# Attention numerators with the query features as stationary operand, tails and query projections in strips

## The chip, the cores and the metric

The kernel runs on one core of one Trainium2 chip. The metric is the device time of one execution in microseconds (us); the kernel before has a median of 1146.33 us over three runs.

## What is computed

Linear attention with positive random features for 8 batches of 8 heads (576 tokens, head size 64, 128 projected features), then a gated feed-forward network (FFN) over the 4608 tokens that come out:

```python
def phi(x):                                   # 64 -> 128 -> 256 features
    proj = einsum('bhsd,df->bhsf', x, w_phi)
    proj = proj - max(abs(proj), axis=-1, keepdims=True)
    return concatenate([exp(proj), exp(-proj)], axis=-1)
q_p, k_p = phi(q), phi(k)
kv  = einsum('bhsf,bhsd->bhfd', k_p, v)       # the sums
z   = sum(k_p, axis=2)
num = einsum('bhsf,bhfd->bhsd', q_p, kv)      # the numerators
den = einsum('bhsf,bhf->bhs', q_p, z)[..., None] + 1e-06
x   = (num / den) laid out as 4608 tokens x 512
out = (silu(x @ w_gate) * (x @ w_val)) @ w_out     # 512 -> 1536 -> 512
```

## The kernel before

**Order of work.** Every piece of work is a `Step` with an engine, an estimated cost, a rank and the PSUM banks that it takes and gives back. `Plan.run` (line 100) plays the steps through with those costs before anything runs and so fixes each engine's order by hand: TensorE takes the ready step of lowest rank, and FFN products have ranks from 1000 on, so they fill what attention leaves. When nothing is ready TensorE gets a matmul on zeros (line 1484). `STRIPS` (350 ns) is the planner's price of going into strips of the array and out again, `SWITCH` (125 ns) that of going from 64-column to 32-column strips.

**Attention** goes by pairs of heads, 32 in all. Each head has 576 tokens: four tiles of 128 and a tail of 64. The tails of the two heads share one tile. Pairs 0 to 7 are *early*: they run before the FFN has input, with more PSUM banks to use. Pairs 8 to 31 are *late*: they run between FFN products and have three work banks.

- Keys (`keys_of`, from line 433): project, take the largest absolute value, subtract, two exponentials. A late pair projects in row strips (64 rows of the array for one head, 64 for the other, line 485); an early pair multiplies by `wbd`, a block-diagonal matrix that does both heads in one 256-column matmul (line 496). Both are fp32, which takes two instructions for one matmul.
- Sums (`values`, line 535): the features are stationary in two 64-column strips, the values (64 columns and a column of ones for `z`: 65) move. The tail tile has both heads in one matmul of 130 columns, with zeros in the other head's half. ScalarE copies the four sums of 65 columns to `kvs` (line 557).
- Queries, early (line 595): project by `wbd`, largest value, subtract, nine 128x128 transposes on TensorE, exponentials out of PSUM.
- Queries, late (line 642): for each head apart, ScalarE makes a rounded half in 64 partitions and VectorE the rest in the other 64, so that one matmul of 128 rows (in the one-pass type fp32r) does both halves: two matmuls (`wst_hi`, `wst_lo`) for each head and half of the tokens, 288 columns each, eight in all. VectorE transposes and reduces across partitions for the largest value.
- Numerators (`numerators`, line 704): the *sums* are stationary in four 32-column strips (`strips`, line 708), the query features move: 512, 64 and 288 columns, the last for the denominators. For a late pair i the sums of pair i+1 run in the same TensorE step just ahead (`merged`). The result has features in partitions and tokens in columns, as the FFN wants it.
- Division (lines 731 to 759): ScalarE copies denominators and numerators out, VectorE transposes the denominators, takes the reciprocal, GpSimd spreads it in six copies (line 748), VectorE transposes it back over 576 columns and multiplies 576 columns.
- Output (line 775 on): for the first four chunks of 384 tokens ScalarE and VectorE make a rounded half `xh` and a rest `xl`; all others go to `x_dram` by one DMA a pair.

**FFN.** Every product is three matmuls in fp32r (hi*hi, hi*lo, lo*hi): `matmuls` (line 354), for later chunks line 1112 and 1359. The weights arrive as 64-bit numbers, and ScalarE and VectorE turn them into halves (`weight_piece`, line 362) while the first FFN products run, up to about 285 us.

Of the kernel before, what the change touches and what calls it, by code (L numbers as in the profile page):

```python
# [10 lines left out]
F32 = mybir.dt.float32  # L11
# [44 lines left out]
ROOM = {"m1": 6912, "m2": 3604, "m3": 2048, "m4": 1152, "a1": 2304, "a2": 2048, "m5": 1024}  # L56
# [167 lines left out]
def favor_attention_moe(ctx: ExitStack, tc: tile.TileContext, qT, kT, v, w_phi, wg, wv, wo, out):  # L224
# [66 lines left out]
    nums = [[view(tag, [S]) for _ in range(2)] for tag in ("m2", "m4")]  # L291
# [3 lines left out]
    rc, rp = sb("rc", [P, NBL]), sb("rp", [P, NBL // 2])  # L295
# [28 lines left out]
    wbd, wst = sb("wbd", [P, 2 * NF]), sb("wst", [P, NF])  # L324
    for h in range(2):
        nc.vector.memset(wbd[h * D:(h + 1) * D, (1 - h) * NF:(2 - h) * NF], 0.0)
        nc.scalar.dma_start(wbd[h * D:(h + 1) * D, h * NF:(h + 1) * NF], w_phi)
# [6 lines left out]
    for h, n in ((h, n) for n in (0, 2) for h in range(2)):  # L334
        if not h:
            nc.gpsimd.memset(vf[n][:, :, :, D:], 1.0)
        nc.gpsimd.memset(vf[n][h * D:(h + 1) * D, 4, 1 - h], 0.0)
        for t in (kin[n], qin[n]):
            nc.gpsimd.memset(t[h * D:(h + 1) * D, 4 * P + (1 - h) * D:4 * P + (2 - h) * D], 0.0)
# [85 lines left out]

    level = lambda i: 2 if i < NPAIR else 1 if i < EARLY_PAIRS else 0
# [7 lines left out]
    def keys_of(i, rank):  # L434
# [10 lines left out]
        if i == EARLY_PAIRS + 1:  # L445
            def clear():
                nc.gpsimd.memset(vf[1]()[:, :, :, D:], 1.0)
                for h in range(2):
                    nc.gpsimd.memset(vf[1]()[h * D:(h + 1) * D, 4, 1 - h], 0.0)
                    nc.gpsimd.memset(kin[1]()[h * D:(h + 1) * D, 4 * P + (1 - h) * D:4 * P + (2 - h) * D], 0.0)  # L450
# [18 lines left out]
        by_head = not early  # L469
        for g, (t0, t1) in enumerate(GROUPS):  # L470

            tail = t1 == 5
            slots = [(4, 0)] if tail else [(t, g) for t in range(4)] if by_head else [(t, h) for t in range(t0, t1) for h in range(2)]
# [5 lines left out]
            def project(t0=t0, t1=t1, key=key, tail=tail):  # L479
                x = get(kin[one])  # L480
                if by_head and not tail:
# [6 lines left out]
                o = work[plan.bank[key]]  # L488
                for t in range(t0, t1):
                    c = slice(t * P, (t + 1) * P)  # L490
                    matmuls([(o[:, :NF], x[:, c], wst, True, True) if tail else
                             (o[:, (t - t0) * 256:(t - t0 + 1) * 256], x[:, c], wbd, True, True)])
# [4 lines left out]
            elif not by_head:  # L497
                kproj = add("PE", 2 * pe32(256), project, after, rk, take=[key])
# [36 lines left out]
        def values():  # L535
            ps_kv = work[plan.bank["kv", i]]
            for g, (t0, t1) in enumerate(GROUPS):
                tail = t1 == 5
                slots = [(4, 0)] if tail else [(t, g) for t in range(4)] if by_head else [(t, h) for t in range(t0, t1) for h in range(2)]
                for m, (t, h) in enumerate(slots):  # L540
                    for k in range(2):
                        x = kp[g][:, m, k]
                        y = get(vf[one])[:, 4].rearrange("p h d -> p (h d)") if tail else get(vf[one])[:, t, h]
                        n = (2 * k + h) * D2
# [8 lines left out]
    def sums_of(i, rank, kv):  # L553
# [4 lines left out]
        kvc = [add("ACT", act(4 * D2), lambda: nc.scalar.copy(kvs[j], work[plan.bank["kv", i]][:, :4 * D2]),  # L558
                   [kv, *use("kvs")], rank, give=("kv", i))]
        last["kvc", i] = kvc[-1]  # L560
        sums[i] = kvc

    def attention(i, rank):
        late = i >= EARLY_PAIRS
        if i <= EARLY_PAIRS:
# [3 lines left out]
            sums_of(i, rank, add("PE", 20 * pe32(D2) // 2 + STRIPS, values, ready,  # L569
                                 rank + (OFFSETS[0] if late else 0), take=[("kv", i)]))  # L570
# [23 lines left out]
        if early:  # L594
            for g, (t0, t1) in enumerate(GROUPS):
                tail = t1 == 5
                w = t1 - t0

                u = 1 if tail else 2 * w
# [5 lines left out]
                def project(t0=t0, t1=t1, key=key, tail=tail):  # L605
                    o = work[plan.bank[key]]
                    for t in range(t0, t1):
                        x = get(qin[one])[:, t * P:(t + 1) * P]
                        matmuls([(o[:, :NF], x, wst, True, True) if tail else
                                 (o[:, (t - t0) * 256:(t - t0 + 1) * 256], x, wbd, True, True)])  # L610

                pj = add("PE", pe32(NF) if tail else w * pe32(256), project, q_in, rank, take=[key])
# [12 lines left out]
                def turn(w=w, y=y, key2=key2, tail=tail):  # L625
                    o = work[plan.bank[key2]]
                    for h in range(1 if tail else 2):
                        for t in range(w):
                            nc.tensor.transpose(o[:, (h * w + t) * P:(h * w + t + 1) * P], y[:, 2 * t + h], ident)  # L629
# [3 lines left out]
                size = D if tail else w * P  # L633

                def exponential(k, t0=t0, size=size, key2=key2):
# [903 lines left out]
```

## Time and profile before

| | us |
|---|---|
| median of 3 runs (1145.62 to 1147.04) | 1146.33 |
| span of the profiled execution | 1143.8 |
| TensorE matmul busy in it | 1129.0 (99%) |
| VectorE busy | 932.6 (82%) |
| ScalarE busy | 613.1 (54%) |
| GpSimd busy | 156.4 (14%) |

The profile shows one execution. "Busy" of TensorE counts the time in which at least one matmul is in the array; matmuls overlap, so the pitch (start to start) tells what one costs, and not its duration. The median lies 2.5 us above the span, which is what lies around the span.

### The profile page before, as it was taken

The numbers are of one execution on the slowest core, as the hardware profiler recorded it, in microseconds if no ns is written. First come the engines' busy times: TensorE is split into PE (matmuls) and PEld (weight loads), VectorE is DVE, ScalarE is ACT, GpSimd is POOL, SyncE is SP. The second block draws the span as 40 slices with busy tenths as digits, with TensorE's granted clock in tenths as the row PEclk, the third lists the DMA queues.
The fourth block names the chain that finished last, engine by engine and source line by source line (L and its number), as shares of the span: only waits on it lengthen the run. The fifth ranks groups of instructions, "written<-read, shape, count | busy, mean of one in ns | idle before, by whom it ended". The sixth has DMA issues, their size and how long they took to land.

```text
span 1143.8 us, 25584 instructions
## 1 busy us (share of the span) xinstructions
PE 1129.0 (99%) x9842; PEld 1015.4 (89%) x9842; DVE 932.6 (82%) x1478; ACT 613.1 (54%) x1263; POOL 156.4 (14%) x385
## 2 busy tenths in 40 slices
PE   9999999999999999999999999999999999999998
PEld 7677999998777788888889988988999999999998
DVE  5999999998888788899889989986756566988663
ACT  6776333335766655676567655744434344544342
POOL 1111000002232323312311011010132000000000
PEclk9999999999999999999999999999999999999999
DMA  6546777856788776889988887877799878642511
GB/s 174 151 111 223 286 285 285 284 206 212 226 243 265 259 258 228 281 264 328 320 272 272 293 283 237 257 231 253 269 297 321 266 252 293 222 163 87 180 42 42
DMA packets 161705, 269.47 MB, mean 236 GB/s; under 512 B 56496, under 2 KB 106800, under 8 KB 158512
## 3 DMA queue, kind: packets, MB, share of 16 engines
q1 hardware_dynamic: 161120, 267.64, 71.0%
q8 instruction: 78, 1.28, 0.5%
q14 instruction: 43, 0.35, 0.1%
q10 hardware_dynamic: 464, 0.20, 0.1%
HBM read 187.56 MB, written 80.22 MB: 234 GB/s over the span
## 4 chain that ended last, share of the span: by engine, by line
PE 91%; DMA 4%; DVE 2%; SPq 1%; POOL 1%; issue 1%; ACT 1%; DVEq 0%; POOLq 0%; ACTq 0%
PE gv L354 17%; PE o L1112 14%; PE gv L1112 14%; PE o L354 10%; PE work L1359 7%; PE work L710 7%; PE work L354 6%; PE work L546 5%; PE gv L1359 5%; PE o L1359 4%; DMA w<-w_dram 2%; PE o L710 1%; PE o L546 1%; PE o L629 1%; DMA h_dram<-m 0%
## 5 line engine op out<-in xcount | busy, mean ns | idle before, releaser
L354 PE MATMUL gv<-xh,w 128*128 128x384 f32 x768 | 207.3, 338 | 3.0 <-DVE m L863 3.0
L354 PEld LDWEIGHTS gv<-xh,w 128*128 128x128 f32 x768 | 139.8, 188 | 7.4 <-DVE m L863 3.7
L354 PE MATMUL gv<-xl,w 128*128 128x384 f32 x384 | 128.7, 335 | 0.0
L354 PE MATMUL o<-w_hi,hidden 128*128 128x512 f32 x288 | 100.8, 400 | 0.0
L1112 PE MATMUL gv<-xh,w 128*128 128x384 f32 x336 | 98.8, 339 | 1.8 <-DVE w_hi L1231 1.1
L1112 PE MATMUL o<-m,w 128*128 128x384 f32 x388 | 80.8, 336 | 0.2 <-ACT snap L1122 0.2
L710 PE MATMUL work<-m,m 128*32 128x64 f32 (+2 forms) x1248 | 79.0, 400 | 0.0
L354 PEld LDWEIGHTS gv<-xl,w 128*128 128x128 f32 x384 | 72.1, 188 | 1.4 <-DVE xl L784 0.2
L1112 PEld LDWEIGHTS o<-m,w 128*128 128x128 f32 x388 | 68.4, 188 | 1.4 <-ACT snap L1122 0.6
L354 PEld LDWEIGHTS o<-w_hi,hidden 128*128 128x128 f32 x288 | 54.0, 188 | 14.3 <-issue 3.7
L710 PEld LDWEIGHTS work<-m,m 128*32 128x32 f32 x1248 | 30.2, 110 | 40.8 <-issue 34.4
L1112 PEld LDWEIGHTS gv<-xh,w 128*128 128x128 f32 x336 | 61.9, 188 | 4.8 <-issue 1.9
L1125 DVE TENSOR_TENSOR snap<-o,snap 128x384 f32<-128x384 f32 x72 | 39.9, 554 | 25.5 <-PE o L1112 20.4
L354 PE MATMUL o<-w_lo,hidden 128*128 128x512 f32 x144 | 56.8, 394 | 0.0
L1112 PE MATMUL o<-xh,w 128*128 128x384 f32 x188 | 54.9, 338 | 1.7 <-DMA w<-w_dram 1.7
L1112 PE MATMUL gv<-xl,w 128*128 128x384 f32 x168 | 56.4, 336 | 0.0
L1125 DVE TENSOR_TENSOR snap<-gv,snap 128x384 f32<-128x384 f32 x72 | 39.8, 552 | 20.2 <-PE gv L1112 14.0
L1122 ACT COPY snap<-o 128x384 f32<-128x384 f32 x72 | 34.3, 476 | 39.8 <-PE o L1112 25.8
L1122 ACT COPY snap<-gv 128x384 f32<-128x384 f32 x72 | 34.2, 475 | 36.7 <-PE gv L1112 21.2
L861 ACT ACTIVATE m<-gv 128x384 f32<-128x384 f32 x36 | 17.6, 490 | 66.3 <-PE gv L354 65.4
L531 ACT ACTIVATE m<-m 128x512 f32<-128x512 f32 (+1 forms) x88 | 45.7, 519 | 10.7 <-DVE m L507 10.6
L693 ACT ACTIVATE m<-m 128x576 f32<-128x576 f32 x48 | 31.4, 690 | 37.3 <-DVE m L686 37.3
(423 smaller groups left out, 3096.0 us busy)
## 6 DMA issues: line engine op xcount, KB each, us to landing
w<-w_dram SPq DMA_DIRECT2D x113, 512.0 KB, 5.6
h_dram<-m SPq DMA_DIRECT2D x90, 192.0 KB, 5.2
w_dram<-w SPq DMA_DIRECT2D x12, 1024.0 KB, 6.3
w_dram<-a SPq DMA_DIRECT2D x24, 512.0 KB, 4.4
w<-w_dram SPq DMA_DIRECT2D x12, 1024.0 KB, 6.8
w<-w_dram SPq DMA_DIRECT2D x38, 256.0 KB, 4.4
w_lo<-w_dram SPq DMA_DIRECT2D x36, 256.0 KB, 3.4
spare<-h_dram SPq DMA_DIRECT2D x19, 384.0 KB, 3.9
```

Source lines behind the costliest of these rows:

```text
L354: nc.tensor.matmul(o, l, r, start=a, stop=z)
L531: e0 = add("ACT", act(n * NF), lambda x=room: nc.scalar.activation(x[:, :, 0], x[:, :, 1], AF.Exp), after, rk)
L546: nc.tensor.matmul(ps_kv[r, n:n + (2 if tail else 1) * D2], x[:, r], y, start=g + m + k == 0, stop=tail and k == 1)
L629: nc.tensor.transpose(o[:, (h * w + t) * P:(h * w + t + 1) * P], y[:, 2 * t + h], ident)
L693: f0 = [add("ACT", act(S), f, [qc], rm) for h, f in enumerate(per_head(lambda h: nc.scalar.activation(qe[j][:, h], qx[j][:, h], AF.Exp)))]
L710: strips = lambda o, c, l, x, n, begin, final: nc.tensor.matmul(o[32 * n:32 * n + 32, c], l, x, start=begin, stop=final)
L861: s1 = add("ACT", act(CH), lambda: nc.scalar.activation(get(t_), ps_gv[0][:, :CH], AF.Tanh, scale=0.5), [ends[0], th_free[j]], FIRST)
L1112: nc.tensor.matmul(o[:, :CH], l, r, start=begin and i == 0, stop=i == len(terms) - 1, skip_group_check=True)
L1122: return add("ACT", act(CH), lambda: act_.copy(snap[n], bank[:, :CH]), [after, *snap_free[n]], FIRST)
L1125: return add("DVE", dve(CH), lambda: vec.tensor_tensor(out=snap[n], in0=bank[:, :CH], in1=snap[n], op=ALU.add), after, FIRST)
L1359: nc.tensor.matmul(cut(o, t - ts[0], W), l, r, start=begin and q == 0 and m == 0 and t == ts[0], stop=q == NQ - 1 and m == 2, skip_group_c ...
```

## The change

- Numerators: the query features become stationary, 64 tokens in each of two 64-column strips, and the sums of 65 columns move. One matmul form now gives numerators and denominator, with tokens in partitions: 36 matmuls a pair. ScalarE adds 1e-6 to the 5 (or 4) denominators of a partition, VectorE takes one reciprocal over nine columns and multiplies 320 and 256 columns out of PSUM.
- The result then has to be turned: four 128x128 transposes on TensorE and, for the tails, two fp32 matmuls against the identity in quarters of the array (64 rows by 64 columns), into two PSUM banks one after the other. The halves `xh`/`xl`, or a copy for `x_dram`, are made out of PSUM.
- The tail of the sums: eight matmuls in quarters of the array in place of four of 130 columns; each head's sums go to a bank of their own, and ScalarE copies them in two pieces. For a late pair they share the two banks of the numerators, so the step takes two banks in place of three.
- Early projections of keys and queries: row strips as for late keys; `wbd` and its two loads go.
- Late queries: one rounded half and one rest over 128 partitions (both heads at once), then per half of the tokens three matmuls (hi*hi, hi*lo, lo*hi) for each head in a row strip of 64 rows, twelve in all. Both heads' banks are taken together.
- The transposes back and forth of the denominators and GpSimd's six copies go.

```diff
@@ values (sums) @@
+    SUMS_COST = 18 * pe32(D2) // 2
-                        for r in (slice(0, P // 2), slice(P // 2, P)):
-                            nc.tensor.matmul(ps_kv[r, n:n + (2 if tail else 1) * D2], x[:, r], y,
-                                             start=g + m + k == 0, stop=tail and k == 1)
+                        for c in halves:
+                            nc.tensor.matmul(o[c, n:n + D2], kp[h][:, t, k, c], get(vf[one])[:, t, h],
+                                             start=t + k == 0, stop=False)
+            for k in range(2):
+                n = at + k * D2
+                for c in halves:
+                    for h in range(2):
+                        r = rows(h)[0]
+                        nc.tensor.matmul(work[plan.bank[names[h]]][c, n:n + D2], kp[2][r, 0, k, c], get(vf[one])[r, 4, h],
+                                         start=False, stop=alone and k == 1)
@@ early queries (keys alike) @@
-                                 (o[:, (t - t0) * 256:(t - t0 + 1) * 256], x, wbd, True, True)])
+                    for t in range(4):
+                        for h in range(2):
+                            r = rows(h)[0]
+                            matmuls([(work[plan.bank["q", i, h]][:, t * NF:(t + 1) * NF], x[r, t * P:(t + 1) * P],
+                                      wst[r], True, True)])
@@ late queries @@
-                        x = qs()[:, h, c]
-                        matmuls([(acc, wst_hi, x, True, False), (acc, wst_lo, x, False, True)])
-                    pj = add("PE", 2 * pe(SH), project, [lo, *use("qx")], rq, take=[key])
+                    for n, (w, x) in enumerate(((wst_hi, 0), (wst_hi, 1), (wst_lo, 0))):
+                        for h in range(2):
+                            r = rows(h)[0]
+                            nc.tensor.matmul(work[plan.bank[keys[h]]][:, :SH], w[r], qs()[r, x, c], start=n == 0, stop=n == 2)
+                pj = add("PE", 3 * pe(SH) + STRIPS, project, [q_lo, *use("qx")], rq, take=keys)
@@ numerators @@
-                    strips(oa, slice(0, WIDE), kvs[j][:, at:at + 32], (qe, qx)[k][j][:, n // 2, :WIDE],
-                           n, k == 0, k == 1)
...
+                for t in range(4):
+                    for k in range(2):
+                        for c in range(2):
+                            n = starts[t] + c * D
+                            nc.tensor.matmul(o[c * D:(c + 1) * D, t * D2:(t + 1) * D2], (qe, qx)[k][j][:, h, n:n + D],
+                                             kvs[j][:, (2 * h + k) * D2:(2 * h + k + 1) * D2],
+                                             start=not merged and t + k == 0, stop=h == 1 and t == 3 and k == 1)
...
+        nu = add("PE", SUMS_COST + STRIPS + (SUMS_COST if merged else 0), numerators,
+                 [*done, *kvc, *(made_keys[i + 1][1] if merged else ())], rn, take=names)
@@ division @@
-        t0 = add("DVE", dve(SH), lambda: vec.transpose(turned, den[:, :SH]), [c_den], rt)
-        ts = add("POOL", 6 * 230, spread_out, [t1, last.get(("num'", i - 1))], rt)
-        t2 = add("DVE", dve(S), lambda: vec.transpose(
-        t3 = add("DVE", dve(S), lambda: vec.tensor_tensor(out=num, in0=num, in1=den, op=ALU.mult), [t2, *c_num], rt)
+        t1 = add("DVE", 210, lambda: vec.reciprocal(r_, r_), dens, freeing)
+        scaled = [add("DVE", dve((5 - h) * D), lambda h=h: vec.tensor_tensor(
+            out=y[:, :5 - h, h], in0=slots_of(h)[:, :, :D], op=ALU.mult,
+            in1=r_[:, 5 * h:9 if h else 5].rearrange("p (t o) -> p t o", o=1).broadcast_to([P, 5 - h, D])),
+                      [t1, held_by[h]], freeing, give=names[h]) for h in range(2)]
@@ turned output @@
+            def turn(n=n, parts_=parts_):
+                o = work[plan.bank["x", i, n]]
+                for m, t in enumerate(parts_):
+                    if t < 4:
+                        nc.tensor.transpose(o[:, m * P:(m + 1) * P], y[:, t].rearrange("p h d -> p (h d)"), ident)
+                        continue
+                    for h in range(2):
+                        r = rows(h)[0]
+                        nc.tensor.matmul(o[r, m * P:m * P + D], y[r, 4, 0], ident[r, r], start=True, stop=True)
+            turns.append(add("PE", 108 * len(parts_) + STRIPS // 2 * (4 in parts_), turn, scaled, rt, take=[("x", i, n)]))
```

## Rows read from the trace of the kernel before

**Rows 1.** The page, part 1: busy us, share of the span, instructions.
```profile
PE 1129.0 (99%) x9842; PEld 1015.4 (89%) x9842; DVE 932.6 (82%) x1478; ACT 613.1 (54%) x1263; POOL 156.4 (14%) x385
```
**Rows 2.** Busy by stretch: PE, PEld, DVE, ACT, POOL (instructions), granted clock, DMA share, GB/s.
```profile
30.00:40.00 10.00, 8.99 (x141) 6.60 (x142) 9.00 (x19) 7.12 (x23) 2.22 (x6) 1.00 0.30 79
...
110.00:120.00 10.00, 7.09 (x39) 6.78 (x40) 9.65 (x14) 3.83 (x6) 0.00 (x0) 1.00 0.85 259
...
300.00:400.00 100.00, 100.00 (x1033) 75.22 (x1027) 83.84 (x131) 66.59 (x146) 29.05 (x66) 1.00 0.80 250
```
**Rows 3.** What TensorE waited for up to 125 us: total, times, longest.
```profile
PE gv L354 <- DVE m L863: 3.0, 2, 1.6
PE gv L354 <- DVE m L507: 1.4, 1, 1.4
```
**Rows 4.** Groups by line and form, sums and zeros: count, busy us, mean ns, idle before.
```profile
L546 PE MATMUL work<-m,m 128*64 128x65 f32 x896 | 29.2, 223 | 0.0
...
L1484 PE MATMUL gv<-nil 128*128 128x256 f32 x33 | 8.0, 382 | 1.1 <-DVE nil L323 1.1
```
**Rows 5.** Timeline of TensorE, sums and numerators of a late pair: start, us, instruction, count.
```profile
315.04 0.40 PE L354 MATMUL o<-w_hi,hidden 128*128 128x512 f32 x1
315.36 2.53 PE L546 MATMUL work<-a,m 128*64 128x65 f32 x72
317.82 3.12 PE L710 MATMUL work<-m,m 128*32 128x512 f32 x48
320.87 0.51 PE L354 MATMUL o<-w_hi,hidden 128*128 128x512 f32 x1
321.21 0.39 PE L354 MATMUL o<-w_lo,hidden 128*128 128x512 f32 x1
```
**Rows 6.** The same timeline cut at 316.67 us: the sums' first 44 instructions.
```profile
315.36 1.50 PE L546 MATMUL work<-a,m 128*64 128x65 f32 x44
```
**Rows 7.** The timeline behind it: key projection in row strips, query projection among FFN.
```profile
322.84 0.39 PE L354 MATMUL o<-w_hi,hidden 128*128 128x512 f32 x1
323.16 1.58 PE L354 MATMUL work<-wst,m 64*128 64x128 f32 x18
324.50 0.48 PE L354 MATMUL o<-w_hi,hidden 128*128 128x512 f32 x1
324.82 0.39 PE L354 MATMUL o<-w_lo,hidden 128*128 128x512 f32 x1
...
326.45 0.40 PE L354 MATMUL o<-w_hi,hidden 128*128 128x512 f32 x1
326.68 0.30 PE L354 MATMUL work<-a,wst_hi 128*128 128x288 f32 x1
326.82 0.29 PE L354 MATMUL work<-a,wst_lo 128*128 128x288 f32 x1
```
**Rows 8.** Timeline of TensorE, early stage: projections by `wbd`, transposes, tail projection.
```profile
63.33 1.03 PE L354 MATMUL work<-wbd,m 128*128 128x256 f32 x4
64.19 1.03 PE L354 MATMUL o<-wbd,m 128*128 128x256 f32 x4
...
90.96 0.60 PE L629 MATMUL o<-ident,m 128*128 128x128 f32 x4
91.40 0.39 PE L354 MATMUL work<-wst,m 128*128 128x128 f32 x2
```
**Rows 9.** VectorE groups up to 112 us: line, form, count, busy us, mean ns.
```profile
L757 DVE STREAM_TRANSPOSE m<-rc 128x576 f32<-128x576 f32 x8 | 6.2, 776 | 3.4 <-POOL rc L753 3.4
L759 DVE TENSOR_TENSOR m<-m 128x576 f32<-128x576 f32 x8 | 6.1, 759 | 0.8
L743 DVE STREAM_TRANSPOSE m<-m 128x288 f32<-128x288 f32 x8 | 3.8, 473 | 0.2
...
L507 DVE TENSOR_TENSOR m<-work,km 128x512 f32<-128x512 f32 x4 | 2.8, 689 | 0.1
...
L507 DVE TENSOR_TENSOR m<-work,km 128x128 f32<-128x128 f32 x5 | 1.4, 290 | 0.1
```

More of the change, by code (lines that the diff above doesn't have):

```diff
@@ L480, in project @@
                 x = get(kin[one])
-                if by_head and not tail:
+                if not tail:
                     for t in range(4):
@@ L487, in project @@
                     return
[L488 to L492, printed above, removed]
+                matmuls([(work[plan.bank[key]][:, :NF], x[:, 4 * P:5 * P], wst, True, True)])
             after = [*k_in, last.get(("kv", i - (2 if early else 1)))]
@@ L551, in keys_of, with sums_of @@
         plan.early = 0
[L553 removed]
+    def sums_of(i, rank, kv, names, at, own):
         j = i % 2
@@ L594, in attention @@
         if early:
[L595 to L599, printed above, removed]
+            f1s = []
+            for g in range(3):
+                tail = g == 2
+                u = 1 if tail else 4
                 n = 3 * i + g
@@ L706, in numerators @@
+        odd = b % 2
+        starts = (0, 3 * D, 5 * D, 7 * D, 2 * D) if odd else (0, 2 * D, 4 * D, 6 * D, 8 * D)
+        NEXT_AT = 5 * D2 + 3
+        slots_of = lambda h: work[plan.bank[names[h]]][:, :(5 - h) * D2].rearrange("p (t d) -> p t d", d=D2)
         def numerators():
             if merged:
-                made_keys[i + 1][0]()
-            oa, ob = (work[plan.bank[key]] for key in keys)
-            strips = lambda o, c, l, x, n, begin, final: nc.tensor.matmul(
-                o[32 * n:32 * n + 32, c], l, x, start=begin, stop=final)
@@ L727, in attention @@
-        nu = add("PE", pe32(WIDE) * 2 + pe32(SH) * 2 + 300 + STRIPS + (20 * pe32(D2) // 2 + SWITCH if merged else 0), numerators,
-                 [*done[0], *done[1], *kvc, *free, *(made_keys[i + 1][1] if merged else ())], rn, take=keys + [("kv", i + 1)] if merged else keys)
+                made_keys[i + 1][0](names, NEXT_AT, False)
+            for h in range(2):
+                o = work[plan.bank[names[h]]]
+                for t in range(4):
+                    for k in range(2):
[4 more added lines that the diff above has]
+                                             start=not merged and t + k == 0, stop=h == 1 and t == 3 and k == 1)
@@ new lines, in attention @@
+        last["y", i] = turns
+        last["num", i] = []
+        held = [c >= PAIRS for c, *_ in cuts]
+        copied = []
+        for n, (c, at, start, width, _) in enumerate(cuts):
+            src = lambda n=n, width=width: work[plan.bank["x", i, n]][:, :width]
+            if held[n]:
+                copied.append(add("ACT", act(width), lambda src=src, start=start, width=width: nc.scalar.copy(
+                    num[:, start:start + width], src()), [turns[n], *last.get(("num", i - 1), ())], freeing, give=("x", i, n)))
```

195 lines of the change are left out of this document (77 added, 118 removed).

## The prediction

> **What bounds the kernel now.** I read the page's busy shares first: a matmul is in TensorE's array 99% of the span, and no other engine is over 82% [rows 1]. The view by stretches says whether that holds everywhere. From 300 to 400 us, among the late pairs, TensorE is busy for all of 100 us at a granted clock of 1.00, the 2.4 GHz level, while VectorE has 16 us free [rows 2]. Since matmuls overlap, "busy" could still hide a slow pitch, so I went to TensorE's timeline: there FFN products start every 0.23 us up to the block of a pair and again right behind it [rows 5, 7]. Late attention therefore costs the end what it takes on TensorE, and nothing else. The early stage is different. There VectorE is busy 9.0 of 10 us and TensorE only 8.99 [rows 2]; TensorE waits 3.0 us for VectorE's FFN gate and 1.4 us for its key subtraction [rows 3], and runs 33 matmuls on zeros, 8.0 us [rows 4], about half of them before the first data. What can be recovered there is some 8 us: these 4.4, about 2 of zeros between the pairs, and single short waits.
>
> So the sum is TensorE's work, late and early, less what VectorE's relief gives back early. It is made against the span of 1143.8 us; the median is 2.5 us above that.
>
> **Prices.** *64-column strips, 65 moving columns:* 44 instructions end 1.50 us after the first start [rows 6], one lasts 0.22 [rows 4], so 43 pitches take 1.28: 0.030 each with a slow first one, 0.029 behind it, 0.058 for the two strips side by side. *A 128-column fp32 instruction:* four transposes from 90.96 to 91.40, 0.11 each [rows 8]. *A visit to row strips:* the key projection of a late pair takes from 323.07 (322.84 plus a pitch) to 324.59 (324.82 less a pitch), 1.52 us [rows 7]. Its 16 strip instructions, two side by side, are 8 x 0.11 and its tail 2 x 0.11: 1.10. So two strips do run side by side (one by one it would be 1.98), and the visit costs 0.42 over its columns; I take 0.40, or 0.20 a change of layout. *Column strips to others:* the sums take 2.46 us to the numerators' start [rows 5]; 32 pairs at 0.058 and four of 130 columns at 0.11 are 2.30, so this change costs 0.16. Changes to and from quarters of the array are not in the trace; I take 0.17, between these two. The bounds are 0.05 (the slow first pitch of strips alone) and 0.20.
>
> The Trainium skill, "TensorEngine Tiling (Array Packing)", section Performance Considerations, speaks against the numerators' new form: it gives each matmul some 60 cycles of overhead and advises against tiling a dimension that is small already. At 2.4 GHz that would be 0.025 us (an estimate from that page) on each of the 72 new instructions, 1.8 us more a pair if nothing overlapped. The trace disagrees: the same form runs at a pitch of 0.029 us all told [rows 6].
>
> **A late pair, part by part.**
> - *Sums and numerators.* Before: from 315.27 to 320.98, 5.71 us with all changes [rows 5]. After: 32 strip pairs of the sums and 36 of the numerators (36 matmuls are 72 instructions, two strips side by side) are 68 x 0.058 = 3.94. The sums' tail is 16 instructions in quarters: four at a time 0.23, two at a time 0.46; I take 0.23, since row strips and column strips both go side by side [rows 6, 7]. Four changes (in, quarters, back, out) are 0.68. Together 4.85: **0.86 less**; 0.63 less with the tail two at a time.
> - *Query projection.* Before: eight matmuls at a pitch of 0.135 [rows 7], 1.08, among FFN products without a change of layout. After: both heads take banks together, two of the three, so the halves of the tokens can't follow each other at once, and each is a visit: 0.40 + 3 x 0.135 = 0.81, twice 1.61: **0.53 more**. Fp32r in row strips is not in the trace. If strips ran one by one it would be 2 x (0.40 + 6 x 0.135) = 2.42, 1.34 more; a cheaper visit (0.30) gives 0.33 more. I take side by side, by the key projection, the nearest row.
> - *Turning the output.* Four transposes are 0.44, the tail's four instructions in quarters 0.12, the changes into quarters and out 0.38: **0.94 more**; 0.66 with changes at 0.05.
>
> Sum: -0.86 + 0.53 + 0.94 = +0.61 us, for 24 pairs **+14.6 us**. (Pair 31 has no merged sums: its numerators go from 3.25 to 36 x 0.058 + 0.36 = 2.45, much the same gain.)
>
> *Beside that, at no cost:* VectorE loses two transposes and a product, 0.47 + 0.78 + 0.76 [rows 9], and one of two query subtractions, and gains two products out of PSUM of 320 and 256 columns: by the slope between 128 and 512 columns, (689 - 290)/384 = 1.04 ns a column, 0.49 and 0.42 [rows 9]. It has room anyway [rows 2]. ScalarE makes one rounded half in place of two, copies the sums in two pieces, and queues the two small copies of denominators; GpSimd's six copies go. The DMA of a pair to `x_dram` stays one, and SyncE's queue keeps its order. New waits: the turned output waits on TensorE for both products, with FFN steps to fill; ScalarE's small copies wait for the numerators, and behind them stand its FFN copies, for which TensorE's next product on that bank waits. The planner doesn't price the quarters in the numerators and prices the turned tail at half, so TensorE would run some 0.5 us a pair behind the plan. With FFN from two banks in turn I take nothing for it; the high side is 0.3 us a pair, 7 us.
>
> **An early pair.** Projections: four `wbd` instructions take 0.86 [rows 8], so eight are 1.72, with the tail 1.94; in strips 1.52. That is 0.42 less, twice, for keys and queries: -0.84. Sums: tail 0.44 to 0.23, one change more: -0.04. Numerators: 3.05 with 0.20 at the edges, 3.25 [rows 5], to 2.45: -0.80. Turning: +0.94. Sum -0.74, for eight pairs **-5.9 us**. Transposes of the query features stay nine. VectorE: -2.01 + 0.91 = -1.10 a pair, -8.8 us in the stage that it nearly binds [rows 2, 9]. That is enough to follow TensorE's shorter work and to give back part of the 8 us of waits; not all, because the 3.0 us at the FFN gate [rows 3] come when VectorE also turns out weights, which doesn't change. I take **-4.5**, between 0 and -8.
>
> **Sum.** +14.6 - 5.9 - 4.5 = +4.2 us: span 1148.0, median **1150.5 us**, 0.4% slower. The change shortens the numerators as it is meant to, but TensorE pays it back in layout changes: per late pair three (in, to 32 columns, out) and two for the keys become four, two, four for the queries and two for the turned tail.
>
> **Rivals.**
> - *Quarters cost little to enter* (faster). Each pair has four changes into or out of quarters, two in the sums and two at the turned tail: 128 in all, priced at 0.17. The forecast turns to a gain as soon as one costs 0.033 less, under 0.14. At half, 0.085, the sum is 4.2 - 128 x 0.085 = -6.7: 1139.6. For it: a column-strip change shows only 0.16 with its slow first pitch, and quarters may reuse 64-column strips. Against: every boundary between layouts that the timeline has adds at least 0.09 before the first matmul [rows 5, 7].
> - *The early stage gives all back* (no change). If VectorE alone held the early stage, 8 us go instead of 4.5: +0.7, 1147.0. For it: 9.65 of 10 us busy at 110 us [rows 2]. Against: TensorE is full there too but for the waits.
> - *Fp32r strips don't run side by side* (slower by much, and the query part doesn't do what it says). +0.81 a pair, 24 pairs: +19, 1170. Against: fp32 strips do [rows 7], and the type changes the passes, not the layout.
> - *The order planned with wrong prices stalls TensorE*: +7, 1157.5.
>
> The Trainium skill, "TensorEngine Tiling (Array Packing)", section Key Properties, says that changing the tiling mode, not the tile alone, drains TensorE. Boundaries of 0.32 us where the pitch is 0.23 [rows 5, 7] agree; whether quarters drain alike no row here shows, and by that rule the first rival falls.
>
> **How the numbers follow.** The forecast with its small errors (about 1147 to 1156) has 0.41 of the chance, cheap quarters 0.29, the early stage giving all back 0.17, wrong prices 0.06, fp32r one by one 0.07. What a measurement of this kernel can tell from no change is 0.2%, 2.3 us. The forecast leaves some chance to each side: 0.04 of it lies within 2.3 us; the early rival reaches 0.02 to the faster side. So faster 0.31, within 0.19, slower 0.50. Cases of both signs hold much, so the range goes from cheap quarters at half price (1139) to wrong prices and part of one-by-one strips (1165); the forecast's own range is 1147 to 1156.
>
> **What would show it.** In the profile after: numerators of 72 instructions at a pitch of 0.029; a sums-and-numerators block of 4.85 us where 5.71 stood; two query visits of 0.8 a late pair, each three pitches long; transposes at 0.11 with a visit of about 0.5 at the tail; FFN pitch still 0.23; fewer zeros and waits before 125 us. I am wrong if the boundary at quarters is under 0.1, if twelve query matmuls take six pitches a visit, or if TensorE shows waits among the late pairs.

## The result: 0.6% slower, and the profile after

The median is 1154.28 us over four runs (1153.36 to 1155.37), that of the kernel before 1146.68 in the same session: a ratio of 1.0059, interval [1.0041, 1.0076] (taken over all runs; the two medians alone give 1.0066). The profiled execution spans 1152.6 us, 8.8 more than the one before; the forecast was 4.2 more. The sign came out as forecast, and so did the late pairs; the two terms of the early stage did not.

The page of the kernel after, part 1 (busy us, share, instructions), stands against [rows 1]:

```profile
PE 1136.6 (99%) x11364; PEld 1056.2 (92%) x11364; DVE 883.1 (77%) x1420; ACT 591.5 (51%) x1283; POOL 96.6 (8%) x187
```

VectorE, ScalarE and GpSimd lost 50, 22 and 60 us of work, as the change means them to. TensorE gained 7.6, and it is the engine that sets the end. Where it gained them the timeline of a late pair shows (start, us, instruction, count), against [rows 5, 7]; line 351 is the FFN, 533 and 540 the sums and their tail, 716 and 722 the numerators and theirs, 656 the query projection, 751 and 755 the turning:

```profile
304.02 0.40 PE L351 MATMUL o<-w_hi,hidden 128*128 128x512 f32 x1
304.35 0.53 PE L656 MATMUL work<-a,wst_hi 64*128 64x288 f32 x4
304.72 0.29 PE L656 MATMUL work<-a,wst_lo 64*128 64x288 f32 x2
304.94 0.50 PE L351 MATMUL o<-w_hi,hidden 128*128 128x512 f32 x1
305.28 0.40 PE L351 MATMUL o<-w_lo,hidden 128*128 128x512 f32 x1
...
308.39 0.40 PE L351 MATMUL o<-w_hi,hidden 128*128 128x512 f32 x1
308.72 2.09 PE L533 MATMUL work<-a,m 128*64 128x65 f32 x64
310.74 0.46 PE L540 MATMUL work<-a,m 64*64 64x65 f32 x16
311.13 2.09 PE L716 MATMUL work<-m,m 128*64 128x65 f32 x64
313.05 0.40 PE L722 MATMUL work<-m,m 128*64 128x65 f32 x8
313.38 0.50 PE L351 MATMUL o<-w_hi,hidden 128*128 128x512 f32 x1
313.71 0.40 PE L351 MATMUL o<-w_lo,hidden 128*128 128x512 f32 x1
...
315.35 0.39 PE L351 MATMUL o<-w_hi,hidden 128*128 128x512 f32 x1
315.58 0.60 PE L751 MATMUL work<-ident,m 128*128 128x128 f32 x4
316.11 0.33 PE L755 MATMUL work<-ident,m 64*64 64x64 f32 x4
316.37 0.50 PE L351 MATMUL o<-w_hi,hidden 128*128 128x512 f32 x1
316.71 0.40 PE L351 MATMUL o<-w_lo,hidden 128*128 128x512 f32 x1
```

Each block is read from the end of the FFN product ahead (its start and a pitch of 0.23) to the start that the next FFN product would have had (the start of the second one less 0.23):

- sums and numerators, 308.62 to 313.48: 4.86 us, 5.71 before;
- a query visit, 304.25 to 305.05: 0.80, twice a pair, 1.60 against 1.08 before;
- turning, 315.58 to 316.48: 0.90, nothing before.

Together 7.36 against 6.79: 0.57 us more a pair, 13.7 for 24.

For the whole span I set the start of the n-th FFN matmul (a full-array matmul of 256, 384 or 512 columns; each kernel has 5112) in one timeline against that in the other. This is worked out from the timelines, not an answer of the profile; starts count from the span's start, and the differences are taken before rounding:

```
n-th FFN matmul     0     120     480     720  |  3000    4680
before, us       74.9   126.4   191.0   234.3  | 853.3  1088.6
after, us        60.4   119.8   185.8   229.1  | 863.1  1097.8
after - before  -14.6    -6.6    -5.2    -5.2  |  +9.7    +9.2
```

From the 420th to the 780th matmul, when all early attention is done and no late pair has begun, after leads by a steady 5.2 us. Behind the last late pair it trails by 9.0 to 9.7. So the late pairs cost 14.2 to 14.9 (forecast 14.6), and the early stage brought 5.2, where the forecast had 5.9 + 4.5 = 10.4. That is the error of the sum.

The same timelines show what the 5.2 are made of. I charge each TensorE instruction with the time to the start of the next one, less idle time, and add up to the start of the 420th FFN matmul, us:

```
                        before    after
attention's matmuls       89.3     80.4
FFN matmuls (420)         76.9     78.7
zeros                      7.1      8.9
idle (1.1 at the start)    6.7      6.7
sum                      180.0    174.8
```

Attention's own work shrank by 8.9 us, more than the 5.9 of the forecast; nothing of the waits came back; and 3.7 were lost on FFN matmuls that ran slower and on more zeros.

TensorE's waits in the first 125 us (in all, times, longest; the two largest), against [rows 3]:

```profile
PE gv L351 <- DVE m L856: 3.0, 2, 2.1
PE o L751 <- DVE m L736: 2.2, 2, 1.6
```

The FFN gate (line 856) still costs 3.0, and the turning (line 751) has a new wait of 2.2 for VectorE's scaled products. The sum of TensorE's busy time over the first 250 us, before and after:

```profile
sum 250.00, PE 243.30; mean PE 48.66
```
```profile
sum 250.00, PE 243.27; mean PE 48.65
```

Idle time is 6.70 before and 6.73 after: not a tenth of a microsecond came back. Two small losses come on top. The view by stretches of after (PE, PEld, DVE, ACT, POOL with counts, granted clock, DMA share, GB/s), and the zeros, those ahead of and between attention's steps and those that the plan puts among the FFN, against [rows 4]:

```profile
100.00:110.00 10.00, 7.02 (x53) 6.27 (x50) 8.58 (x12) 3.94 (x7) 0.00 (x0) 0.97 1.02 342
110.00:120.00 10.00, 10.00 (x49) 9.59 (x48) 8.81 (x15) 3.18 (x5) 0.00 (x0) 0.86 0.75 282
```
```profile
L1477 PE MATMUL gv<-nil 128*128 128x256 f32 x41 | 8.0, 350 | 1.3 <-DVE nil L324 1.1 <-DVE m L497 0.3
L1480 PE MATMUL o<-nil 128*128 128x256 f32 x11 | 1.9, 280 | 0.0
```

TensorE idles 2.98 of the ten microseconds from 100, and the granted clock is 0.97 there and 0.86 in the next ten, part of the time at the 1.2 GHz level in place of 2.4. Before, TensorE idled 2.91 us from 110 to 120 at a granted clock of 1.00 [rows 2]. The lower clock costs 0.3 + 1.4 = 1.7 us, which is nearly all that the 420 FFN matmuls take longer. Zeros are 52, where before had 34: the 11 at the FFN's bank all lie ahead of the 420th FFN matmul, where before had none; three of them in a row take 0.36 us, so eleven are 1.3. The 41 others (33 before) take 0.5 more.

### The profile page after: what moved, and what is told of

Read it like the earlier page. It is cut to its first block, busy times and chain, and to the rows that moved or that the text cites. A ratio compares the mean times of both kernels' runs of the same rounds, so it can differ in the third digit from the quotient of the medians.

```text
span 1152.6 us, 28397 instructions
## 1 busy us (share of the span) xinstructions
PE 1136.6 (99%) x11364; PEld 1056.2 (92%) x11364; DVE 883.1 (77%) x1420; ACT 591.5 (51%) x1283; POOL 96.6 (8%) x187
## 4 chain that ended last, share of the span: by engine, by line
PE 90%; DMA 4%; DVE 3%; ACT 1%; issue 1%; POOL 1%; SPq 0%; POOLq 0%; DVEq 0%; ACTq 0%
PE gv L351 18%; PE gv L1105 13%; PE o L1105 13%; PE o L351 10%; PE work L1352 7%; PE gv L1352 4%; PE o L1352 4%; PE work L716 4%; PE work L533 4%; PE work L351 3%; PE work L656 2%; DMA w<-w_dram 2%; PE work L751 1%; DMA m<-w_whole 1%; DMA w_dram<-a 1%; PE work L540 1%
## 5 line engine op out<-in xcount | busy, mean ns | idle before, releaser
L351 PE MATMUL gv<-xh,w 128*128 128x384 f32 x768 | 212.9, 343 | 3.0 <-DVE m L856 3.0
L351 PE MATMUL o<-w_hi,hidden 128*128 128x512 f32 x288 | 103.6, 407 | 0.0
L1105 PE MATMUL gv<-xh,w 128*128 128x384 f32 x336 | 100.4, 342 | 2.0 <-DMA w<-w_dram 2.0
L716 PE MATMUL work<-m,m 128*64 128x65 f32 x1664 | 54.6, 223 | 0.0
L1125 ACT ACTIVATE m<-snap 128x384 f32<-128x384 f32 x47 | 24.7, 525 | 58.0 <-DVE snap L1118 52.2
L716 PEld LDWEIGHTS work<-m,m 128*64 128x64 f32 x1664 | 50.9, 138 | 1.8 <-issue 0.2
L492 DVE TENSOR_REDUCE km<-work 128x4 f32<-128x512 f32 (+1 forms) x85 | 46.9, 552 | 7.3 <-PE work L351 6.8
L958 POOL TENSOR_TENSOR m<-m 128x256 f32<-128x256 f32 x48 | 39.0, 812 | 147.2 <-DMA m<-w_whole 106.5
```

Of the source, the lines that this page charges most:

```text
L351: nc.tensor.matmul(o, l, r, start=a, stop=z)
L492: kmax = add("DVE", dve(n * NF), lambda m=m, view=view: vec.tensor_reduce(out=m, in_=view(), axis=AX.X, op=ALU.max, apply_absolute_value=T ...
L716: nc.tensor.matmul(o[c * D:(c + 1) * D, t * D2:(t + 1) * D2], (qe, qx)[k][j][:, h, n:n + D], kvs[j][:, (2 * h + k) * D2:(2 * h + k + 1) * D2],
L958: done = [add("POOL", POOLED, lambda o=o, l=l, r=r: gp.tensor_tensor(out=x(o), in0=x(l), in1=x(r), op=ALU.subtract), done, rank)]
L1105: nc.tensor.matmul(o[:, :CH], l, r, start=begin and i == 0, stop=i == len(terms) - 1, skip_group_check=True)
L1125: t0 = add("ACT", act(CH), lambda: act_.activation(get(t_), get(x), AF.Tanh, scale=0.5), [*after, th_free[j]], FIRST)
```

## The experiments

Ratios are to the kernel before, timed in the same session (medians 1146.5, 1146.8 and 1146.0). After itself stands at 1.0059. Since every edit makes the planner write another order for all engines, I read each run also by the FFN matmuls as above, from its span's start: at the 420th to 780th (early stage), at about the 3000th (behind the late pairs), and behind that.

**The late queries undone.** They go back to eight full-array matmuls a pair:

```diff
-                    for n, (w, x) in enumerate(((wst_hi, 0), (wst_hi, 1), (wst_lo, 0))):
-                        for h in range(2):
-                            r = rows(h)[0]
-                            nc.tensor.matmul(work[plan.bank[keys[h]]][:, :SH], w[r], qs()[r, x, c], start=n == 0, stop=n == 2)
+                        acc = work[plan.bank[key]][:, :SH]
+                        x = qs()[:, h, c]
+                        matmuls([(acc, wst_hi, x, True, False), (acc, wst_lo, x, False, True)])
```

> The changed kernel with the late query projection put back as it was: halves stacked over 128 rows, eight matmuls in the full array, no row strips. Layouts theory: two visits of 0.80 us a late pair become eight pitches of 0.135, 0.52 us less, 24 pairs: 12.5 us less than the changed kernel, about 1142 us, ratio to the kernel before about 0.995. Rival (relief of VectorE and of the banks sets the pace of late attention): VectorE gets 0.75 us a pair back, so no gain, ratio 1.006 or more.

Measured: 1141.58 us, 0.9954 [0.9938, 0.9971], 12.7 less than after. By the blocks, 24 x (1.60 - 1.08) = 12.5. By the FFN matmuls it gains 14.1 on after from the 780th to the 3000th, of which 2.0 is less idle time of TensorE. Six of the old matmuls in a row in its timeline (the first of them and the FFN products around them):

```profile
300.83 0.40 PE L351 MATMUL o<-w_hi,hidden 128*128 128x512 f32 x1
301.06 0.30 PE L351 MATMUL work<-a,wst_hi 128*128 128x288 f32 x1
...
301.87 0.40 PE L351 MATMUL o<-w_hi,hidden 128*128 128x512 f32 x1
```

They fit between FFN products without an extra gap: 301.06 to 301.87, 0.135 each, and 0.23 from the FFN product to the first. Meanwhile VectorE got its second query subtraction back, so the rival that relief of VectorE sets the late pace falls. The banks are not told apart by this run, since the old form also takes one bank at a time and not two; but TensorE is busy for all of 300 to 400 us in after, so it waits for none there. Without this one part the change is faster than the kernel before.

**The sums' tail last.** It follows the numerators, so that the quarters are entered from the numerators' strips and left straight for the FFN, one change of layout fewer in 23 pairs:

```diff
-                made_keys[i + 1][0](names, NEXT_AT, False)
+                made_keys[i + 1][0](names, NEXT_AT, False, 0)
...
+            if merged:
+                made_keys[i + 1][0](names, NEXT_AT, True, 1)
```

> The changed kernel with one edit of order: in the merged step of a late pair the sums' tail in quarters of the array comes after the numerators and not between the sums and the numerators. The same matmuls, one change of layout fewer in 23 pairs. Layouts theory: 0.15 us a pair, 3.4 us less, ratio about 1.003. Rival (quarters reuse the 64-column strips, and what is paid is the leaving of strips): no difference, ratio 1.006.

Measured: 1150.43 us, 1.0031 [1.0019, 1.0042], 3.8 less than after. Its timeline:

```profile
307.53 0.40 PE L351 MATMUL o<-w_hi,hidden 128*128 128x512 f32 x1
...
311.98 0.46 PE L542 MATMUL work<-a,m 64*64 64x65 f32 x16
312.37 0.50 PE L351 MATMUL o<-w_hi,hidden 128*128 128x512 f32 x1
312.71 0.40 PE L351 MATMUL o<-w_lo,hidden 128*128 128x512 f32 x1
```

The block takes from 307.76 to 312.48, 4.72 us where after takes 4.86. One change fewer is worth 0.14 to 0.15 a pair, 3.2 to 3.5 us in all; the total agrees within its interval.

**Tails turned in the full array.** VectorE writes the tails block-diagonally, and one matmul against two stacked identities turns both:

```diff
-                    for h in range(2):
-                        r = rows(h)[0]
-                        nc.tensor.matmul(o[r, m * P:m * P + D], y[r, 4, 0], ident[r, r], start=True, stop=True)
+                    nc.tensor.matmul(o[:, m * P:m * P + D], y[:, 4].rearrange("p h d -> p (h d)"), stack, start=True, stop=True)
```

> The changed kernel with the tails of the output turned without quarters of the array: VectorE writes the two heads' tails into a block-diagonal tile (two small products more a pair), and one fp32 matmul against two stacked identities, 64 columns, in the full array turns both. Layouts theory: the turning of 0.90 us a pair becomes 0.55, 24 late pairs give 8.4 us, the early ones 0 to 2.8: 1144 to 1146 us, ratio 0.996 to 0.999. Rival (the price of turning is the transposes and the waits on VectorE, not the change of layout): within 2 us of the changed kernel, ratio 1.004 to 1.008.

Measured: 1151.75 us, 1.0042 [1.0027, 1.0058], only 2.5 less, so by the total near the rival's figure. The block itself got shorter, though by less than the 0.35 that I expected; its timeline:

```profile
343.07 0.41 PE L355 MATMUL o<-w_hi,hidden 128*128 128x512 f32 x1
343.31 0.60 PE L760 MATMUL work<-ident,m 128*128 128x128 f32 x4
343.75 0.33 PE L762 MATMUL work<-stack,m 128*128 128x64 f32 x2
343.89 0.47 PE L355 MATMUL o<-w_hi,hidden 128*128 128x512 f32 x1
344.21 0.40 PE L355 MATMUL o<-w_lo,hidden 128*128 128x512 f32 x1
```

Turning takes from 343.30 to 343.98, 0.68 where after takes 0.90, or 5.3 us for 24 pairs. At the 2940th FFN matmul this kernel leads after by 10.5 us, 8.1 of them since the 780th (3.1 of these are less idle time); at the 3180th by 3.1. Between these two stands the longer of two waits of TensorE for FFN weights (total, times, longest), shown with the stretch around it:

```profile
PE gv L1112 <- DMA w<-w_dram: 6.7, 2, 5.5
```
```profile
860.00:870.00 10.00, 10.00 (x60) 10.00 (x59) 4.95 (x9) 4.07 (x10) 0.00 (x0) 1.00 0.98 303
870.00:880.00 10.00, 4.54 (x21) 4.25 (x20) 6.21 (x12) 4.05 (x8) 0.00 (x0) 0.83 0.88 297
880.00:890.00 10.00, 10.00 (x50) 10.00 (x50) 5.67 (x10) 3.54 (x8) 0.00 (x0) 0.83 0.35 129
```

The FFN weights come back from DRAM late, with the DMA engines at a share of 0.98, and the granted clock is 0.83 in the wait's stretch and in the one behind it. So the gain was made and then given back at a transfer.

**The same with weights asked for earlier.** One number more, how many microseconds of planned FFN work ahead of its use a group of loads may be issued:

```diff
-AHEAD = (10, 8, 10)
+AHEAD = (10, 8, 16)
```

> The kernel with the tails turned in the full array, where 7.5 us of the gain were given back at a TensorE wait for FFN weights from 850 to 890 us, with one number changed: these weights may be loaded 16 us and not 10 us ahead of their use. If that wait comes from the place of the load in SyncE's queue, it goes and the gain of some 9 us against the changed kernel shows, 1145 us, ratio 0.998. If it comes from the load on the DMA engines (share 0.98 in those 10 us), it stays or moves, ratio 1.003 to 1.005.

Measured: 1149.82 us, 1.0023 [1.0008, 1.0039], between the two. The wait of 5.5 us is gone: between 850 and 930 us TensorE waits for no weights but 3.4 us in two waits that the profile puts down to ScalarE's copies of partial sums, and the granted clock stays at 1.00. So the loads' place in the queue does set the wait for weights. At this place the kernel loses 3.5 us (a lead over after of 6.4 at the 3000th FFN matmul, of 2.9 at the 3180th), where without the number it lost 7.4. The 4 us that this saves had been lost ahead of it: 1.8 of them by the first FFN matmul, ahead of which its granted clock is 0.83 from 20 to 30 us (1.00 without the number). The intervals of the two kernels overlap: on the total this run is inconclusive.

**All three.** The edits of the first three runs together.

> The three edits together: late queries in the full array, tails turned in the full array, sums' tail last. Layouts theory: the savings add, 12.5 + 8.4 + 3.4 = 24 us less than the changed kernel, about 1130 us, ratio 0.985: faster than both kernels. Rival (a new bound, VectorE or the pace of late attention, takes over once TensorE is relieved): less than half of it, ratio above 0.995.

Measured: 1137.56 us, 0.9921 [0.9901, 0.9941]: 16.7 less than after, where the three alone sum to 19.0 and I expected 24: between the two theories. That the sum comes near is in part luck, since turned tails alone lost 7.4 us at the weights and this kernel loses 3.4. At the 3000th FFN matmul the three alone lead after by 14.7 + 3.8 + 10.5 = 29.0, and together by 20.9. Most of these 8 us is idle time of TensorE from the 780th to the 2940th: 5.5 us in after, 3.5, 5.3 and 2.4 in the three alone, whose savings together would leave next to none, and 7.6 here. The turning waits for VectorE's products, 4.6 us in all among the late pairs, where after has no such wait. The kernel beats both others.

**Late queries undone and the sums' tail last.**

> The changed kernel with the late queries back in the full array and the sums' tail after the numerators; the output tails stay in quarters. Layouts theory: the two savings add, 12.7 + 3.9 us less than the changed kernel, about 1138 us, ratio 0.992. Rival (an attention pace that another engine sets): less than the first alone, ratio 0.995.

Measured: 1138.54 us, 0.9926 [0.9909, 0.9943]. The two gains sum to 16.5; 15.7 are there. This too beats both kernels, and its early waits are those of after (2.8 and 2.2).

**The early projections undone.** They leave the strips for the block-diagonal matrix, which by the forecast gives TensorE 6.9 us of work back:

```diff
-                            matmuls([(work[plan.bank["k", i, h]][:, t * NF:(t + 1) * NF], x[r, t * P:(t + 1) * P],
+                            matmuls([(work[plan.bank["k", i, h]][:, t * NF:(t + 1) * NF], x[:, t * P:(t + 1) * P],
+                                      wbd[:, h * NF:(h + 1) * NF], True, True) if early else
...
-                            matmuls([(work[plan.bank["q", i, h]][:, t * NF:(t + 1) * NF], x[r, t * P:(t + 1) * P],
-                                      wst[r], True, True)])
+                            matmuls([(work[plan.bank["q", i, h]][:, t * NF:(t + 1) * NF], x[:, t * P:(t + 1) * P],
+                                      wbd[:, h * NF:(h + 1) * NF], True, True)])
```

> The changed kernel with the early projections of keys and queries out of row strips again: full-array matmuls against block-diagonal weights, 128 columns for each head, 0.43 us more TensorE work per projection, 16 projections, 6.9 us. Theory A (TensorE binds the early stage): all of it shows, ratio to the kernel before about 1.012, 1161 us. Theory B (VectorE, with the first weights to turn out, binds it, and TensorE's early savings go into waits): 0 to 2 us, ratio 1.005 to 1.008.

Measured: 1163.24 us, 1.0146 [1.013, 1.0162]. The total speaks for one theory and its place for the other. The first FFN matmul comes 3.2 us later than in after, but the 420th to the 840th come at the same time. Up to there attention's matmuls take 89.3 us, 8.9 more than in after: all of it went back in at no cost. Part of where it went shows in the same sum over the first 250 us:

```profile
sum 250.00, PE 245.93; mean PE 49.19
```

Idle time is 4.07 in place of 6.73, zeros are 22 in place of 52 (4.5 us in place of 8.9), and the granted clock is 1.00 from 100 to 150 us. So TensorE's amount of work does not set when the 420th FFN matmul comes. The 9 us of the total arise later: 5.6 of them at FFN weights around 870 us (one wait of 4.5), as in the run with turned tails.

**VectorE relieved.** The clamp of the weights' magnitudes is left out, one VectorE pass of each weight piece (that part of the computation is missing):

```diff
-        s1 = add("DVE", dve2(n), lambda: vec.tensor_scalar(
-            out=e(), in0=e(), scalar1=F64_LEAST, scalar2=F64_MOST, op0=ALU.max, op1=ALU.min), [s0], rank)
+        s1 = s0
```

> The changed kernel without VectorE's clamp of the magnitudes in the conversion of the FFN weights from 64 bits (one step of seven, 0.68 us on 1024 columns and 0.42 on 512; it acts only on magnitudes outside the 32-bit range). 1.1 us less VectorE work per piece pair, 12 of them, up to about 285 us; TensorE's work is the same. Theory B (VectorE binds the early stage): 2 to 6 us less than the changed kernel, ratio 1.000 to 1.004, all of it before the first 285 us. Theory A (TensorE binds): within 1 us of it, ratio 1.005 to 1.007.

Measured: 1165.18 us, 1.0167 [1.0146, 1.0189], slower with a step less. The first FFN matmul is 2.9 us earlier, but the 60th 4.4 later, and from the 180th to the 480th it is 1.5 to 2 later. The gate still makes TensorE wait 3.1 us, the longest 2.5. But the run doesn't test what it was made for: up to the 420th FFN matmul VectorE is busy for 158.0 us, in after for 154.4. The plan used the room to bring weight steps forward (84.4 us of them up to there, in after 79.4), so VectorE was not relieved there. What less work on VectorE would bring in an unchanged order stays untested. Again 6.7 us of the total arise at a wait for FFN weights near 870 us, 5.7 long.

**Weight steps planned longer.** Both runs also rewrote the order, so I looked at the order itself. In after, the gate's steps stand in VectorE's and ScalarE's queues behind steps of the weights. VectorE and ScalarE ahead of the longer wait:

```profile
105.12 1.22 DVE L391 TENSOR_TENSOR a<-a 128x1024 f32<-128x1024 f32 x1
107.45 1.23 DVE L394 TENSOR_TENSOR w<-a,w 128x1024 fp32r<-128x1024 f32 x1 [1.11 <-ACT w L393]
108.59 0.55 DVE L856 SCALAR_TENSOR_TENSOR m<-m,gv 128x384 f32<-128x384 f32 x1
```
```profile
106.37 1.05 ACT L393 CAST w<-a 128x1024 fp32r<-128x1024 f32 x1 [4.62 <-DVE a L391]
107.33 0.48 ACT L854 ACTIVATE m<-gv 128x384 f32<-128x384 f32 x1
```

ScalarE stands still for 4.62 us until VectorE's line 391 is done, converts weights (line 393), and only then takes the gate's tanh (line 854); VectorE stands for 1.11, finishes the weights (line 394), and then comes to the gate (line 856), for which TensorE waits. The plan counts on these weight steps to be over by then. So I changed their estimate alone, for the seven VectorE steps of a piece:

```diff
+LATE_WEIGHTS = 1.15
-        s1 = add("DVE", dve2(n), lambda: vec.tensor_scalar(
+        s1 = add("DVE", LATE_WEIGHTS * dve2(n), lambda: vec.tensor_scalar(
```

> After, with one number of the planner changed: the VectorE steps that turn out the FFN's weights are planned 15% longer than they are. No work changes, only the order that the planner writes out for each engine. Theory order: TensorE's early waits for the FFN gate (3.0 us, the longest 2.1) come because the gate stands behind a weight step that VectorE or ScalarE can't begin yet; planned longer, the weight steps go behind the gate more often. Then these waits fall under 1.5 us and the FFN products from the 420th to the 780th start 1.5 to 3 us earlier than in after: about 1152, ratio 1.004, if nothing later changes. Theory amount: VectorE has too much to do before 125 us in any order. Then the waits move but their sum stays above 4 us and these products start within 0.7 us of after's: about 1154, ratio 1.006. The wait for FFN weights from DRAM between 860 and 925 us can add or take some 5 us to the total in either case, so the place is read and not the total alone.

Measured: 1156.03 us, 1.0075 [1.0048, 1.0102]: no gain in total. At the place the theory holds, though not to its numbers (1.8 at the gate against under 1.5, and 5.1 us earlier at the 420th FFN matmul against 1.5 to 3):

```profile
PE gv L352 <- DVE m L857: 1.8, 2, 1.1
PE o L752 <- DVE m L737: 1.2, 2, 0.6
```
```profile
100.00:110.00 10.00, 8.24 (x46) 7.85 (x46) 9.08 (x13) 3.55 (x6) 0.00 (x0) 1.00 1.04 333
110.00:120.00 10.00, 10.00 (x57) 9.59 (x56) 9.38 (x15) 4.21 (x8) 0.00 (x0) 1.00 0.88 336
```
```profile
L1481 PE MATMUL o<-nil 128*128 128x256 f32 x35 | 5.8, 281 | 0.0
```

The two waits are 3.0 us in place of 5.2, the granted clock stays at 1.00 there, and the 300th FFN matmul starts 4.8 us earlier than in after, the 420th 5.1. Of the 5.1, idle time gives 1.6, the FFN matmuls 1.3, zeros 1.2 and attention's matmuls 1.0. Against before that makes 10.3, the forecast's 10.4, but by other terms: 9.9 on attention's matmuls and 1.6 of idle time, less 1.2 for zeros and FFN matmuls. VectorE's work isn't smaller, but its weight steps come later: up to the 420th it is busy for 145.6 us, in after for 154.4, and 69.1 and 79.4 of these are weight steps. Then the same longer estimate makes the plan put 35 zeros among the FFN, 24 more, 18 of them between the 420th and the 780th (2.1 us), so at the 780th 2.9 are left. The late pairs cost more here, and why stays open: behind them this kernel trails after by 2.6.

**The same on the best two edits.**

> The late queries undone and the sums' tail last (1138.5 us, 0.9926), with the same change of the planner's number: weight steps planned 15% longer. Theory order: 1.5 to 3 us less, about 1136, ratio 0.991. Theory amount: within 1 us of 1138.5, ratio 0.9926. Again a changed wait for FFN weights between 860 and 925 us could hide either in the total.

Measured: 1140.7 us, 0.9955 [0.9933, 0.9976], against 0.9926 without it; the total is neither theory's. The early lead is there again (5.9 us at the 420th, 3.7 at the 780th, of which 0.3 at the first), and again gone at the 3000th (1.6 behind).

## Why the prediction was right, and where its sum was off

- **What bounds.** Right. TensorE is busy for all of 300 to 400 us before and after, and what a late pair takes on it reached the end whole: 0.57 x 24 = 13.7 from the blocks, 14.2 to 14.9 by the FFN matmuls. 2.3 of the 14.9 are idle time (5.5 us from the 780th to the 3000th, 3.2 before), most of it waits for FFN weights around 800 us, for which the forecast had nothing; that 14.6 was met so closely is in part luck.
- **Sums and numerators.** -0.86 forecast, -0.85 measured. Quarters run four at a time: the tail's sixteen instructions start within 310.74 + 0.46 - 0.23 = 310.97, 0.23 us from the first. Into them it takes 0.15 (the last strip instruction starts at 308.72 + 2.09 - 0.22 = 310.59, the quarters at 310.74), out of them 0.16; I took 0.17. Both measured figures hold a pitch of the matmul ahead, 0.03 for a strip and 0.015 for a quarter, so the changes alone are 0.12 and 0.14. That the block comes out at 4.86 all the same is due to strips that run at 0.030 each and not 0.029.
- **Query projection.** +0.53 forecast, +0.52 measured. The strips run side by side in fp32r too: six matmuls in three pitches. Undoing it gave back 12.7 us.
- **Turning.** +0.94 forecast, +0.90 measured.
- **The early pairs' work, -5.9, and the waits given back, -4.5.** Together -5.2 was measured, and both terms were off. The work shrank by 8.9 and not 5.9, mostly by the projections: 33.8 us before and 24.5 after up to the 420th FFN matmul, 9.2 less where the forecast had 0.84 x 8 = 6.7. (The four `wbd` instructions of [rows 8] have a pitch of 0.215; all 128 have 0.224.) Numerators (-6.3), sums (-0.6) and turning (+7.1) came as forecast, within half a microsecond. The step that failed is the other one: "enough to follow TensorE's shorter work and to give back part of the 8 us of waits". It gave back 0.0 (6.70 to 6.73 us idle), and 1.8 us of zeros and 1.9 of slower FFN matmuls came on top, for which the forecast had nothing: it looked for fewer zeros and got 52 in place of 34. -8.9 + 1.8 + 1.9 is the -5.2. I read the waits as VectorE having too much to do. But VectorE's own busy time up to the 420th fell by 4.8 (159.2 to 154.4), not by the 8.8 of the forecast: after's order puts 3.5 us more of weight steps ahead of it (75.8 to 79.4). What the runs show: 8.9 us more of TensorE's work moved nothing at the 420th, and another order brought 5.1 us there. So up to there the order that the planner writes from its estimates sets the pace. Whether less work on VectorE in the same order would have given the waits back, no run shows.
- **The rivals.** *Quarters cheap to enter* falls: the boundary is 0.15, and one change fewer in the run with the sums' tail last shortened the block by 0.14. The Trainium skill, "TensorEngine Tiling (Array Packing)", Key Properties, has a change of mode drain the array; for quarters the trace now agrees as far as the time goes, with 0.15 where the pitch of these strips is 0.06 for two. *The early stage gives all back* falls with what is said above. *Strips one by one* falls: a visit is 0.80. *Wrong prices stall TensorE* cost little here: from 300 to 800 us TensorE idles 2.0 us against 0.7 before, 1.3 and not 7. But three experiments paid that price, 5.6 to 7.4 us, at a place that I hadn't looked at: the FFN weights' return around 870 us. In after this place happened to cost nothing more than before (the FFN matmuls' distance is 9.7 at the 3000th, 9.1 behind it). The chance of 0.06 that I gave it may have been too small.

So the forecast was right for its main reason, the price of layout changes against shorter columns, and 4.6 us short on the span: the early stage alone brought 5.2 less than forecast.

## What to carry to other kernels

When TensorE sets the end, count the changes of layout before the columns: here one costs 0.12 to 0.20 us, as much as two or three pairs of 65-column strip instructions, and a projection that stays in the full array between FFN products beat one of fewer columns that needs two visits. Relief on an engine need not give back a wait: here VectorE's relief left TensorE's early idle time as it was. Where an order is written by hand, look first at what stands ahead of the awaited instruction in its queue. And when each edit rewrites the whole order, compare kernels at a fixed product along the span, since a total can carry 5 us from a place that the edit never touched.

## What the runs showed of the hardware that I had not expected

Row strips in fp32r run side by side as those in fp32 do: six matmuls of 288 columns in a visit of 0.80 us. Four quarters of the array run at once: sixteen instructions of 65 columns start within 0.23 us. A change between strips and quarters costs nearly the same both ways (0.15 in, 0.16 out). And an idle stretch of TensorE can cost twice: behind single waits of 2.1 us (after) and 5.5 us (turned tails) the granted clock of the next ten microseconds was 0.86 and 0.83. The length of the wait alone doesn't decide it. The run with the late queries undone has the same early waits, one of 1.60 us up to 96.73 and one of 2.15 up to 110.19, and there the clock fell behind the shorter one and not behind the longer:

```profile
90.00:100.00 10.00, 8.40 (x158) 7.53 (x156) 9.72 (x20) 7.66 (x17) 0.00 (x0) 0.91 0.89 324
100.00:110.00 10.00, 7.40 (x66) 6.51 (x62) 7.48 (x9) 3.57 (x7) 0.00 (x0) 0.92 0.98 299
110.00:120.00 10.00, 9.81 (x53) 9.41 (x54) 9.72 (x17) 3.56 (x6) 0.00 (x0) 1.00 0.87 317
```
